# Sharing the last shifted reading of the exponential between VectorE and GpSimd, with other planner constants and another tail, in a one-core transformer block

## The chip, the core and the metric

The kernel runs on one core of a Trainium2 chip. The time is device microseconds (us) of the core for one execution, here the median of 3 runs. Engines: TensorE (PE in the profile), VectorE (DVE), ScalarE (ACT), GpSimd (POOL) and SyncE (SP), which issues the DMAs.

## What is computed

One block with adaptive layer norm: 2048 rows of 512, 32 heads of 16, then a dense layer of 1376 with gelu. Inputs are bf16.

```python
mod = (silu(c) @ w_mod).reshape(1, 6, 1, 512)   # sa, ca, ga, sb, cb, gb
h = layernorm(x) * (1 + ca) + sa
q, k, v = heads(h @ wqkv)                        # 32 heads of 16
p = softmax(q k^T / 4)
x = x + ga * ((p v) @ wo)
h = layernorm(x) * (1 + cb) + sb
x = x + gb * (gelu(h @ w1 + b1) @ w2 + b2)
```

## The kernel before

**Tiles.** The rows are cut into four blocks of 512 queries (`NQ`). Attention goes in 32 *runs*: a run is four heads with 512 queries in the first three blocks, and eight heads with 256 queries (two halves of 256 columns) in the last. A run walks over 16 tiles of 128 keys, and a tile has four *score pieces* of 128 keys x 512 columns, so there are 2048 score pieces in all. TensorE makes a piece in a quarter of its rows (L822).

**Two ways to an exponential.** Most pieces go to ScalarE: three pieces, then two, in turn, land in PSUM tiles `st` (one of three banks, one of two), and one exp instruction reads them all and writes `pt` (L871). For up to four key tiles of a run VectorE does it without an exp: a *PSUM pass* (L912) adds a constant to a score piece in PSUM tile `ax`, cuts it off at zero and writes it as int16 into a quarter of `ph`; its bits, read as bf16, are a coarse power of two. Four *shifts* (L927) add a constant to the whole of `ph` (128x2048, int16, SBUF to SBUF) into `sh`. The V product (L960) sums the five readings, each with V scaled to match (`VX`, made by GpSimd in L756), which evens out the coarseness. The four passes and four shifts of one key tile are called a group here. The sum lands in `od`, with a column of ones giving the denominators; VectorE copies it to SBUF (`OD`, L985), the denominators go through DRAM and come back spread, and GpSimd multiplies (L1012).

**What sets the order.** The order of every engine's instructions is found while the program is built, by a planner (`Plan`, L105) that plays the engines forward with a cost for each operation. It picks for each engine the ready operation with the best priority, and which key tiles go to VectorE (`next_tile`, L801) falls out of that. Its constants are the costs: `A_US` (an exp of one, two or three pieces), `AL` (from an exp's cost to the release of its banks), `PEL` (from the matmul's cost to its readers), and `SEEDS`, which breaks near ties, one for every 25 us of planned time. `ahead` (L162) keeps out TensorE work that would make ScalarE's next scores late. Nothing moves at run time: the chip follows these orders and waits on semaphores. An operation marked `port` uses the SBUF port that VectorE's SBUF-to-SBUF shifts and GpSimd are planned to take in turn; `beside` (L175, L1043) lets GpSimd work only while VectorE does something else, and `after_dve` (L1049) ties such a GpSimd instruction to the end of the VectorE instruction before the one last issued.

**Around attention.** `layer_norm` (L635) makes statistics on VectorE, the inverse deviation on GpSimd (L612, L614), and transposes on TensorE, one `ax` bank for each of four column blocks. `block_tail` (L1153) makes a block's output projection, residual, layer norm and dense layer beside the next runs; 11 blocks of 128 of the dense layer, one `ax` bank each (L1183), are moved out by VectorE (L1193) and put through one gelu. For the last block `block_tail` is called for the first 256 rows only. Eight of its dense blocks go that way and three wait for the end of all exps and are read by ScalarE (L1189). Two banks (`ax`) serve all this and VectorE's scores; the other banks are `od` and `st`.

**The tail.** When the last run ends, `last_half` (L1223) finishes the last 256 rows, two tiles of 128: it loads x again, and for each tile transposes `od`, inverts the denominators, multiplies (L1249 to L1256), projects (L1263), adds (L1267), and goes through layer norm (L607 to L618), the dense layer (L1295, L1298, L1123), the last add (L1310) and the store. The second tile's transposes use the same `OD` buffer and wait for the first tile's statistics.

Of the kernel before, what the change touches and what calls it, by code (L numbers as in the profile page):

```python
# [12 lines left out]
ALU = mybir.AluOpType  # L13
# [40 lines left out]
PEL = 0.24  # L54
OVER = 0.0
DVE_PE = 0.0
DL = 0.14
DPL = 0.08
AL = 0.17
FILL = 1.6  # L60
SPREAD = 0.15
SEEDS = (571, 338, 517, 702, 966, 607, 659, 937, 623, 185, 209, 513, 12, 512, 674, 785, 660, 579, 642, 245, 112, 195, 497, 319, 388, 80, 556, 716, 338, 990, 290, 195)
# [11 lines left out]
class Op:  # L74
    count = 0

    def __init__(self, eng, fn, us, deps=(), lat=0.14, prio=5.0, mode=None, kind="", acq=None,
# [10 lines left out]
        self.rows, self.cont, self.run = None, False, None  # L88
# [16 lines left out]
class Plan:  # L105
# [39 lines left out]
    def pick(self, eng):  # L145
# [4 lines left out]
        if eng == "PE":  # L150
            can = self.ahead(can)
# [10 lines left out]
    def ahead(self, can):  # L162
# [4 lines left out]
        limit = max(q[0][0], self.need() - q[0][1].us - PEL - 0.02) + OVER  # L167
# [5 lines left out]
        return keep  # L173

    def beside(self, us):  # L175

        at, end, port = self.dve
        t = max(at, self.now, self.free["POOL"])
        if t >= end:
            nxt = self.pick("DVE")  # L180
            return nxt is None or nxt[0] - t >= us
        return not port and end - t >= us

# [74 lines left out]
def kernel(  # L258
# [34 lines left out]
    MM = 512 / 2400.0  # L293
    SPAN = (3, 2)
    POOL_US, POOL_MIN = 0.68, 0.5
    A_US = {1: 0.49, 2: 0.92, 3: 1.345}
    AHEAD = 3
    PSUM_F = 8
# [50 lines left out]
    def dyn(plan, o):  # L349
        if o.eng == "DVE" and o.run is not None and (  # L350
                o.run < a_run[0] or o.run == a_run[0] and not own[o.run]):
            return 0.05
        if o.eng != "PE":
            return o.prio
# [14 lines left out]
        if o.kind == "last":  # L369
            return o.prio + 0.1 * same  # L370
        if o.due <= prog():
# [263 lines left out]
    def layer_norm(src, deps, mod, mod_dep, hold_z, alloc_h, engines, ps_res, kind, prio,  # L635
# [39 lines left out]
        else:  # L675
            for j in range(NC):
                def tr(o, j=j):
                    o.ps = o.tile.bitcast(BF16)[:, 0:nt * P]
                    for t in range(nt):
                        nc.tensor.transpose(out=o.ps[:, t * P:(t + 1) * P],  # L680
                                            in_=z.tile[:, t, j * P:(j + 1) * P], identity=ident)
                one = op("PE", tr, nt * 0.0705, za, lat=PEL, mode=("full", 0), kind=kind,
                         acq=r_ax, rel=(z,))
                trs.append(one)
                e = engines[j]
                done.append(op(e, lambda o, j=j, one=one, e=e: modulate(
                    e, h.tile[:, j, 0:nt * P], one.ps, mod, j), 0.13 + nt * 0.1, (one, mod_dep, h), prio=0.1,
                    rel=(one,)))
# [144 lines left out]
    def qk_a():  # L833
# [30 lines left out]
        o = op("PE", go, MM, deps, lat=PEL, mode=("qk",) + tuple(u[2] for u in got), kind="qkA", acq=r_st[n],  # L864
# [19 lines left out]
    def qk_d():  # L884
# [29 lines left out]
        d_e.append(op("DVE", ex, 0.61, (o,), lat=DL, prio=0.5, rel=(o,)))  # L914
# [7 lines left out]
    def shifts(r, kt, first, es):  # L922
# [3 lines left out]
        for j in range(1, NPH):  # L926
# [4 lines left out]
            pv_op(r, kt, j, (sh,), parts(sh), (sh,))  # L931

# [50 lines left out]
    def normalise(r):  # L983
# [20 lines left out]
        def d5(o):  # L1004
# [8 lines left out]
            out=OT.tile[:, c], in0=OD.tile[:, c], in1=o5.tile[:, c], op=ALU.mult), (OT,), (OD, o5))  # L1013
# [29 lines left out]
    def beside(fn, deps, rel=(), prio=0.5):  # L1043

        return [op("POOL", lambda o, c=c: after_dve(fn(slice(c * HB, (c + 1) * HB))), POOL_US, deps, lat=0.1,
# [107 lines left out]
    def block_tail(b, nt=TPB):  # L1153
# [19 lines left out]
        if part:  # L1173
            g.uses += 1
            o_late["part"] = g
            one = ones(g, (g,))
        ev = []
        over = op("NIL", None, 0.0, (), lat=0.0, prio=0.0, gate=finished) if part else None
        if part:
            open_banks()  # L1180
        for f in range(NF):
            direct = part and f >= PSUM_F
            mm = chain([(lambda ps, f=f, j=j: nc.tensor.matmul(  # L1183
                out=ps[:, 0:N], lhsT=W1[:, j, f * P:(f + 1) * P], rhs=h.tile[:, j, 0:N],
                start=(j == 0), stop=(j == NC - 1)), nt * MM / NC) for j in range(NC)],
                hd + [o_late["w1"], g, over if direct else None], kind,
                r_t if direct else r_ax, (h,))
            if direct:
# [264 lines left out]
```

## Time and profile before

| What | Value |
|---|---|
| Runs | 788.44 us median, 787.47 to 790.36 |
| Span of the profiled execution, first to last instruction | 785.5 us |
| Median of the runs less that span | 2.9 us |
| Mean granted TensorE clock | 0.996 |
| Busy: PE / DVE / ACT / POOL | 731.1 (93%) / 737.5 (94%) / 756.9 (96%) / 125.0 (16%) us |
| First exp starts, last exp ends | 14.2, 761.0 us |
| Chain that ended last, by engine | ACT 42%, PE 29%, DVE 14%, issue 12%, DMA 2% |

The profile is of one execution. Its own time is its span and what lies around it, which the profile does not give; the median of the runs is the nearest figure. A line of it names the source line, the engine, the operation, the tiles written and read with their shapes and how many there were; then busy time, mean duration in ns, and the idle time of the engine just before these instructions with what ended it. A mean duration runs from an instruction's start to its end, and on VectorE and ScalarE the next one starts before that, so what a long row costs is read from starts, not from means. PE's busy time is modelled and says little of how much room it has.

### The profile page before, as it was taken

The numbers are of one execution on the slowest core, as the hardware profiler recorded it, in microseconds if no ns is written. First come the engines' busy times: TensorE is split into PE (matmuls) and PEld (weight loads), VectorE is DVE, ScalarE is ACT, GpSimd is POOL, SyncE is SP. The second block draws the span as 40 slices with busy tenths as digits, with TensorE's granted clock in tenths as the row PEclk, the third lists the DMA queues.
The fourth block names the chain that finished last, engine by engine and source line by source line (L and its number), as shares of the span: only waits on it lengthen the run. The fifth ranks groups of instructions, "written<-read, shape, count | busy, mean of one in ns | idle before, by whom it ended". The sixth has DMA issues, their size and how long they took to land.

```text
span 785.5 us, 20448 instructions
## 1 busy us (share of the span) xinstructions
PE 731.1 (93%) x8209; PEld 272.8 (35%) x8286; DVE 737.5 (94%) x1285; ACT 756.9 (96%) x683; POOL 125.0 (16%) x279
## 2 busy tenths in 40 slices
PE   8899999999999898999998999999999999999897
PEld 3423333233333222223232233322234343344454
DVE  6779998999999999999999999999899999999974
ACT  4899999999999999999999999999999999999993
POOL 7420224121134300200002000001000100100100
PEclk9999999999999999999999999999999999999999
DMA  7042001001020010001000010001010000101010
GB/s 215 30 138 89 18 23 46 23 16 26 6 71 22 25 42 23 19 22 29 22 23 18 30 34 22 11 16 33 23 57 20 22 20 19 43 18 31 18 44 29
DMA packets 39073, 28.22 MB, mean 36 GB/s; under 512 B 17957, under 2 KB 34374, under 8 KB 38978
## 3 DMA queue, kind: packets, MB, share of 16 engines
q1 hardware_dynamic: 38970, 26.91, 12.0%
q8 instruction: 65, 1.06, 0.6%
q14 instruction: 30, 0.25, 0.1%
q10 hardware_dynamic: 8, 0.00, 0.0%
HBM read 21.30 MB, written 2.61 MB: 30 GB/s over the span
## 4 chain that ended last, share of the span: by engine, by line
ACT 42%; PE 29%; DVE 14%; issue 12%; DMA 2%; SPq 0%; POOL 0%; POOLq 0%; DVEq 0%; ACTq 0%
ACT pt L871 40%; PE od L960 9%; PE st L822 8%; DVE sh L927 6%; DVE ph L912 5%; PE ax L1123 2%; PE ax L822 2%; PE ax L1183 2%; ACT g L1202 1%; PE ax L701 1%; PE ax L431 1%; PE ax L740 1%; DVE ln_s L607 1%; DVE OD L985 1%; PE t L1123 1%
## 5 line engine op out<-in xcount | busy, mean ns | idle before, releaser
L871 ACT ACTIVATE pt<-st 128x1536 bf16<-128x1536 f32 x629 | 715.1, 1308 | 3.9 <-PE ax L822 1.7
L912 DVE TENSOR_SCALAR ph<-ax 128x512 int16<-128x512 f32 x476 | 311.1, 680 | 11.2 <-PE ax L822 9.7
L927 DVE TENSOR_SCALAR sh<-ph 128x2048 int16<-128x2048 int16 x476 | 310.8, 692 | 2.6 <-PE od L960 2.3
L822 PE MATMUL st<-qm,kT 32*128 32x512 bf16 x1572 | 246.8, 384 | 23.9 <-ACT pt L871 18.7
L822 PE MATMUL ax<-qm,kT 32*128 32x512 bf16 x476 | 167.0, 380 | 7.6 <-DVE ph L912 5.6
L960 PE MATMUL od<-sh,VX 128*32 128x512 bf16 (+1 forms) x2400 | 167.5, 340 | 5.4 <-DVE sh L927 4.6
L822 PEld LDWEIGHTS <-kT 32*128 32x128 bf16 x2048 | 81.1, 91 | 239.4 <-issue 230.6
L960 PE MATMUL od<-pt,VEB 128*32 128x512 bf16 (+1 forms) x1960 | 145.3, 342 | 0.3 <-ACT pt L871 0.3
L960 PEld LDWEIGHTS <-VX 128*32 128x32 bf16 x2400 | 60.5, 95 | 86.2 <-issue 75.3
L960 PEld LDWEIGHTS <-VEB 128*32 128x32 bf16 x2560 | 62.5, 96 | 75.6 <-issue 63.8
L1012 POOL TENSOR_TENSOR OT<-OD,RB 128x256 bf16<-128x256 f32 x38 | 27.2, 727 | 316.3 <-DVE sh L927 200.4
L960 PE MATMUL od<-ph,VEB 128*32 128x512 bf16 (+1 forms) x600 | 47.5, 340 | 1.7 <-DVE OD L985 1.4
L1012 POOL TENSOR_TENSOR OS<-OD,RB 128x256 bf16<-128x256 f32 x24 | 17.2, 727 | 156.7 <-DVE sh L927 111.0
L1183 PE MATMUL ax<-blk,W 128*128 128x512 bf16 (+1 forms) x145 | 39.8, 359 | 1.8 <-issue 0.6
L756 POOL TENSOR_SCALAR VX<-VEB 128x128 bf16<-128x128 bf16 x64 | 23.1, 360 | 80.7 <-DVE VEB L633 76.9
L701 PE MATMUL ax<-blk,w 128*128 128x512 bf16 x95 | 31.8, 382 | 3.7 <-DVE blk L626 0.9
L1123 PE MATMUL ax<-w,g 128*128 128x512 bf16 x100 | 29.2, 382 | 1.0 <-DVE ph L912 0.2
L1193 DVE TENSOR_SCALAR g<-ax,b1c 128x512 bf16<-128x512 f32 (+1 forms) x41 | 28.2, 692 | 1.1 <-PE ax L1183 0.7
L607 DVE BATCH_NORM_STATS2 ln_s<-xb 128x6 f32<-128x512 bf16 x32 | 21.6, 675 | 1.2 <-DMA xb<-in_A_x_dram 1.1
L1123 PEld LDWEIGHTS <-g 128*128 128x128 bf16 x176 | 14.0, 97 | 23.2 <-issue 12.7
L985 DVE COPY OD<-od 128x512 f32<-128x512 f32 x31 | 21.1, 681 | 0.7 <-issue 0.5
L1183 PEld LDWEIGHTS <-W 128*128 128x128 bf16 x176 | 14.0, 97 | 20.6 <-issue 14.9
(110 smaller groups left out, 367.5 us busy)
## 6 DMA issues: line engine op xcount, KB each, us to landing
RB<-rn SPq DMA_DIRECT2D x124, 64.0 KB
xb<-in_A_x_dram SPq DMA_DIRECT2D x8, 512.0 KB
out_dram<-o SPq DMA_DIRECT2D x16, 128.0 KB
qm<-qs SPq DMA_DIRECT2D x120, 16.0 KB
W<-in_B_w_dram SPq DMA_DIRECT2D x1, 1376.0 KB
w<-in_A_wqkv_dram SPq DMA_DIRECT2D x3, 384.0 KB
blk<-in_w_mod_dram SPq DMA_DIRECT2D x2, 512.0 KB
xb<-in_w_mod_dram SPq DMA_DIRECT2D x2, 512.0 KB
```

Of the source, the lines that this page charges most:

```text
L607: nc.vector.bn_stats(out=st6, in_=src)
L701: return chain([(lambda ps, j=j: nc.tensor.matmul(out=ps[:, 0:QB], lhsT=w.tile[:, j, cc * P:(cc + 1) * P], rhs=o_h[b].tile[:, j, :], start ...
L822: nc.tensor.matmul(out=o.tile[:, k * QB:(k + 1) * QB], lhsT=kT[cc][kb][rows, ko * P:(ko + 1) * P], rhs=qm.tile[rows, par, :] if hb is None ...
L871: nc.scalar.activation(out=e.tile[:, 0:len(got) * QB], in_=o.tile[:, 0:len(got) * QB], func=ACT.Exp, scale=ESC)
L912: nc.vector.tensor_scalar(out=ph.tile[:, o.row * QB:(o.row + 1) * QB], in0=o.tile, scalar1=PH_B, scalar2=0.0, op0=ALU.add, op1=ALU.max)
L927: sh = op("DVE", lambda o, j=j: nc.vector.tensor_scalar(out=o.tile, in0=first.tile, scalar1=PH_SH[j], scalar2=None, op0=ALU.add), 0.6, es, ...
L960: nc.tensor.matmul(out=o_od[r].tile[32 * i:32 * i + 32, n * HB:n * HB + w], lhsT=v_tile(kt, ph)[:, c0:c0 + 32], rhs=got[i][:, at:at + w], ...
L985: OD = op("DVE", lambda o: nc.vector.tensor_copy(out=o.tile, in_=od.tile), 0.6, (last,), prio=0.0, acq=r_OD, rel=(od,))
L1012: two = beside(lambda c: nc.gpsimd.tensor_tensor(out=OT.tile[:, c], in0=OD.tile[:, c], in1=o5.tile[:, c], op=ALU.mult), (OT,), (OD, o5))
L1123: nc.tensor.matmul(out=ps, lhsT=g[:, f, col:col + P], rhs=rhs, start=(f == 0), stop=(f == NF - 1))
L1183: mm = chain([(lambda ps, f=f, j=j: nc.tensor.matmul(out=ps[:, 0:N], lhsT=W1[:, j, f * P:(f + 1) * P], rhs=h.tile[:, j, 0:N], start=(j == ...
L1193: ev.append(op("DVE", lambda o, f=f, mm=mm: nc.vector.tensor_scalar(out=g.tile[:, f, 0:N], in0=mm.tile[:, 0:N], scalar1=b1c[:, f:f + 1], s ...
```

## The change

- Three of the four shifts of a group stay as they are. The last is shared (`shared_reading`): four candidates of 512 columns are offered to GpSimd, and the rest, whatever is left when VectorE reaches it, to VectorE. The V product of that reading waits for all parts. A piece is planned at 0.86 us, and `fits` admits it only when VectorE's present and next operation leave the port free for 0.8 us.
- Planner constants: `AL` 0.17 to 0.055, a new `PEA` of 0.38 in place of `PEL` for ScalarE's scores, exps of two and three pieces 0.9165 and 1.3435, `MM` 0.2155, 32 other seeds; chains once begun get a higher priority (`cont`).
- `fed`: TensorE work that would let VectorE run out of score pieces is kept back.
- `layer_norm` and `block_tail` put two (or four) blocks into one `ax` bank, where their size allows it.
- The last block's first half sends all 11 dense blocks through VectorE and gelu in SBUF (two blocks, then nine in one instruction); the three that ScalarE read from PSUM are gone.
- `last_half` keeps the x tile that the first half loaded, in place of loading it again, and takes an `OD` buffer for each tile, without the wait for the first tile's statistics. The last tiles' second dense layer goes to an `ax` bank.
- The normalising products of the last run but one may run at any time, not only beside VectorE.

The diff, cut to its core:

```diff
-AL = 0.17
+PEA = 0.38
+AL = 0.055
+FEED = 0.2
...
+    def fed(self, can):
+        q = [(s, o) for s, o in can if o.kind == "qkD"]
+        if not q:
+            return can
+        dry = self.free["DVE"] + sum(o.us for o in self.lists["DVE"])
+        limit = max(q[0][0], dry - q[0][1].us - PEL - DL) + FEED
+        return [(s, o) for s, o in can if o.kind in ("qkA", "qkD") or
+                s + o.us + (0.107 if o.mode[0] != "qk" else 0.0) <= limit]
...
+    def fits(self, us):
+        at, end, port = self.dve
+        t = max(at, self.now, self.free["POOL"])
+        if port and t < end:
+            return False
+        nxt = self.pick("DVE")
+        if nxt is None or nxt[0] - t >= us:
+            return True
+        if t >= end or nxt[0] > end + 0.15:
+            return not nxt[1].port and nxt[0] + nxt[1].us - t >= us
+        return end - t >= us or not nxt[1].port and nxt[0] + nxt[1].us - t >= us
...
-    MM = 512 / 2400.0
+    MM = 0.2155
-    A_US = {1: 0.49, 2: 0.92, 3: 1.345}
+    A_US = {1: 0.49, 2: 0.9165, 3: 1.3435}
+    PIECE = 0.86
+    REST = (4.0, 1.0)
+    PIECE_FIT = 0.8
...
-        for j in range(1, NPH):
+        shared_reading(r, kt, first, es)
+        for j in range(1, NPH - 1):
...
+    def shared_reading(r, kt, first, es):
+        sh = op("NIL", None, 0.0, es, lat=0.0, prio=0.0, acq=r_sh)
+        todo = [0, 1, 2, 3]
+        done = Op("NIL", None, 0.0, (), lat=0.0, prio=0.0, rel=(first,))
+        done.todo = 1
+        def add(eng, n):
+            at = slice(todo[0] * QB, (todo[0] + n) * QB)
+            del todo[:n]
+            return eng.tensor_scalar(out=sh.tile[:, at], in0=first.tile[:, at], scalar1=PH_SH[-1],
+                                     scalar2=None, op0=ALU.add)
+        def part(o):
+            after_dve(add(nc.gpsimd, 1))
...
+        def rest(o):
+            o.us = (0.067, 0.2, 0.335, 0.47, 0.6)[len(todo)]
+            o.waiters.append(done)
+            add(nc.vector, len(todo))
+            drop()
...
+        mine = [op("POOL", part, PIECE, (sh,), lat=0.12, prio=0.8, kind="beside", port=True,
+               gate=lambda: plan.fits(PIECE_FIT)) for _ in range(4)]
+        q = op("DVE", rest, 0.6, (sh,), lat=DL, prio=2.0, port=True)
...
+        pv_op(r, kt, NPH - 1, (done,), src, (sh,))
...
-            direct = part and f >= PSUM_F
...
+        for f0 in range(0, NF, QB // N):
+            fs = range(f0, min(NF, f0 + QB // N))
...
-        xr = load_x(b)
+        x2 = held["x"]
...
-        od, OD, OT = o_od[r], take(r_OD), take(r_OT)
+        od, OT = o_od[r], take(r_OT)
...
+            OD = take(r_OD)
...
-                    (o_last[r], OD, s), prio=0.06 + n)
+                    0.42, (o_last[r], OD), lat=0.03, prio=0.06 + n)
...
-                       kind="last", acq=r_t if f == 0 else None, prio=0.4)
+                       kind="last", acq=r_ax if f == 0 else None, prio=0.4)
```

Line numbers move in the changed kernel: the exp is L903, the PSUM pass L944, a whole shift L960, the shared reading L976, the V product L1036.

## The prediction

> **What bounds the kernel now.** First view: the page's slices, engine by engine, with the costliest groups.
>
> ```profile
> DVE  6779998999999999999999999999899999999974
> ACT  4899999999999999999999999999999999999993
> POOL 7420224121134300200002000001000100100100
> ...
> L871 ACT ACTIVATE pt<-st 128x1536 bf16<-128x1536 f32 x629 | 715.1, 1308 | 3.9 <-PE ax L822 1.7
> L912 DVE TENSOR_SCALAR ph<-ax 128x512 int16<-128x512 f32 x476 | 311.1, 680 | 11.2 <-PE ax L822 9.7
> L927 DVE TENSOR_SCALAR sh<-ph 128x2048 int16<-128x2048 int16 x476 | 310.8, 692 | 2.6 <-PE od L960 2.3
> ...
> L1012 POOL TENSOR_TENSOR OT<-OD,RB 128x256 bf16<-128x256 f32 x38 | 27.2, 727 | 316.3 <-DVE sh L927 200.4
> ```
>
> The reader is to see three things. ScalarE's exps (L871) fill 715.1 us with 3.9 us of idle time before them. VectorE's share, PSUM passes (L912) and shifts (L927), fills 622 us. GpSimd is nearly empty after a third of the span. Second view: the busy time of each engine by stretch of the span (columns: length, PE, PEld, DVE, ACT, POOL).
>
> ```profile
> 300.00:400.00 100.00, 92.82 (x913) 29.34 (x921) 99.12 (x172) 99.75 (x89) 9.84 (x14) 1.00 0.09 24
> 500.00:600.00 100.00, 93.98 (x1032) 31.51 (x1046) 95.69 (x160) 98.77 (x84) 6.48 (x9) 1.00 0.10 29
> 760.00:785.50 25.50, 20.20 (x191) 12.16 (x186) 10.41 (x24) 12.90 (x34) 1.77 (x5) 1.00 0.14 44
> ```
>
> Over 40 to 760 us the idle times of ScalarE in these stretches add up to 3.0 us. The last exp ends at 761.0, and a tail of 24.5 us follows in which ScalarE and VectorE are half empty. So the end is set by the front, the length of ScalarE's queue of exps, its gaps, and the tail; VectorE is close behind in the middle.
>
> **Exps.** The built order, which holds no times, has 484 PSUM passes (476 before), so 8 score pieces leave ScalarE: 313 exps of 1536 columns, 312 of 1024 and one of 512, against 314 and 315. ScalarE's own price, from its order in time:
>
> ```profile
> 700.23 60.76 ACT L871 ACTIVATE pt<-st 128x1536 bf16<-128x1536 f32 x53 [0.31 <-PE ax L822]
> ```
>
> 53 exps, wide and narrow in turn: (60.76 - 1.52) / 26 = 2.28 us a pair; two other such rows give 2.27 and 2.28. (The means of one, 1.520 and 1.096, overlap.) With 1.520 - 1.096 = 0.424 for 512 columns, an exp costs 1.35, 0.93 or 0.50 us. One wide and three narrow go, one of 512 comes: -1.35 - 2.78 + 0.50 = **-3.6 us**. Other ScalarE work ahead of the tail is unchanged. The front is not touched: both orders are the same through the tenth exp.
>
> **VectorE.** Shifts and passes follow each other every 0.60 us. Of 121 groups, 363 shifts stay whole. The 121 last readings are split so: VectorE makes all of 57, three quarters of 22, half of 12, a quarter of 8, none of 22; GpSimd makes 158 pieces. Whole shifts go from 476 to 420: -33.6. 42 part shifts come; they are not in the trace. Between their share of 0.60 (14.7 in all) and 0.60 each (25.2), I take the planner's 0.47, 0.335 and 0.2, 16.0 us, which lies by the share. 8 more passes: +4.8. Net -12.8 us (-14.1 to -3.6). On the path this is worth nothing, since ScalarE ends last; it is what pays for the 8 score pieces and for collisions.
>
> **A piece on GpSimd** (512 columns, int16, one input) is not in the trace either. The nearest rows are these: a stretch in order of time on GpSimd and on VectorE, and two lines' shortest, median and longest times in ns (the count at the end of such a row is of records with a shape and may be short).
>
> ```profile
> 155.24 0.73 POOL L1012 TENSOR_TENSOR OT<-OD,RB 128x256 bf16<-128x256 f32 x1 [16.53 <-DVE sh L927]
> ```
> ```profile
> 155.07 0.68 DVE L912 TENSOR_SCALAR ph<-ax 128x512 int16<-128x512 f32 x1
> 155.68 0.84 DVE L927 TENSOR_SCALAR sh<-ph 128x2048 int16<-128x2048 int16 x1
> ```
> ```profile
> L756 POOL TENSOR_SCALAR VX<-VEB x64: 300/301/741, 16.4 to 231.7; 128x128 bf16<-128x128 bf16 x64
> ```
> ```profile
> L927 DVE TENSOR_SCALAR sh<-ph x476: 622/682/1228, 45.4 to 757.5; 128x2048 int16<-128x2048 int16 x159
> ```
>
> 128 columns take 0.301 and two columns (L612) 0.22, so 512 take 0.54 if the growth goes on, and 1.20 if all of it scales by four. I take 0.86, the planner's own price, near the 0.73 of the row that also reads 512 columns. The first three lines show the danger: GpSimd starts 0.17 us after the pass it goes beside, outlasts it, and the next shift takes 0.84 in place of 0.68. The extremes say the same: a GpSimd scaling of 0.30 has taken 0.74, a shift 1.23. What guards against it is in the built order: no piece has fewer than two VectorE instructions other than shifts (and layer norm's applies) between its place and the next shift. 68 have just two, a window of 1.20, of which 1.03 is left after the start. A piece of 0.86 fits and costs VectorE nothing; one of 1.20 costs 68 x 0.17 = 11.6 us, all that was freed. Behind a piece on GpSimd's own queue stand the normalising products and the layer norms' rstd; it idles hundreds of us before them, so nothing is late. The V product of a shared reading waits for its last piece, and on TensorE the next scores for ScalarE stand behind that.
>
> The Trainium skill, "GPSIMD Engine Reference", opening and section 3.1, speaks against the change: GpSimd is the wrong choice for ordinary elementwise work, and its best one-input loop takes 769 ns for 512 elements. No row here shows that loop. By it the piece would be 0.77, inside the window, and the sum the same. "SBUF — State Buffer", section "Who interferes with whom", says the port shared with VectorE is held for the whole instruction and the other blocks fully. By that the shift above should lose 0.17 + 0.73 - 0.60 = 0.30; it lost 0.16, so a collision costs about half as much here.
>
> **Planner's other constants** (exp to release 0.17 to 0.055, scores to exp 0.24 to 0.38, the rule that keeps VectorE fed, chains with two blocks to a bank, seeds). They add no instruction and reorder TensorE. The trace shows ScalarE waiting for scores seven times, 3.2 us, of which 3.0 of idle time from 40 us on, and TensorE waiting for an exp 67 times, 18.7 us. An order that places scores 0.14 earlier can at best remove the 3.0. At worst gaps come all over as they do from 500 to 700 us (1.9 us in 200): 6.9 over 720 us, +3.9. I take 0, between the two.
>
> **Tail.** These lines of the order in time carry it.
>
> ```profile
> 761.54 0.45 DVE L1249 STREAM_TRANSPOSE OD<-od 128x256 f32<-128x256 f32 x1 [2.52 <-issue]
> ...
> 766.59 0.69 DVE L1267 TENSOR_TENSOR xb<-t,xb 128x512 bf16<-128x512 f32 x1 [3.42 <-DMA xb<-in_A_x_dram]
> ...
> 775.93 2.80 PE L1295 MATMUL t<-blk,W 128*128 128x128 bf16 x44
> ...
> 782.06 0.69 DVE L1310 TENSOR_TENSOR o<-t,xb 128x512 bf16<-128x512 f32 x1 [1.74 <-PE t L1123]
> ```
>
> The first tile's residual add waits 3.42 us for x, which is loaded again; the change keeps x. The second tile's transposes need no longer wait for the first tile's statistics. Against that, 11 first-layer matmuls (0.107 each from a 256-column row's spacing, 1.2 us) now stand ahead of the last V product, which starts the chain about 0.5 us later after the last exp, and the gelu of nine blocks is one instruction: 1.47 + 768 x 0.82 ns = 2.1 us (0.82 ns a column from the 512- and 1536-column gelus, 0.63 and 1.47), with TensorE idle about 1 us before the 9 matmuls that need it. Placing the built order at these rows, counted from the end of the last exp: the first add starts at 3.7 (before 5.6), the second tile's at 9.5 (10.7). Then TensorE is what is late: 22 second-layer matmuls of the first half at 0.213, the first tile's 44 at 0.064 and the rest are in front. The second tile's 44 start at 14.6 (14.9), and 12 second-layer matmuls in place of 15 follow them: -0.3 - 0.6 = **-1.0 us** (0, if nothing passes TensorE, to -1.8, the second add's whole 1.2 and the three matmuls).
>
> **Sum.** 785.5 - 3.6 - 1.0 = 780.9 us of span. The runs' median is 788.44, 2.9 above that span; I keep the 2.9: **783.8 us**, 0.6% below.
>
> **Rivals.** *A, gaps on ScalarE eat it.* The order is new everywhere after the front; at the rate of 500 to 700 us it has +3.9, and with no gain in the tail +1.0: 788.7; with half of each, 786.2. For: one blocked TensorE instruction holds all behind it. Against: 0.4 us of gaps in 400 us from 100 to 500. *B, pieces longer than the plan (slower).* Place: the V product that waits for a shared reading. A piece of 1.20 is 0.34 over 0.86; behind four in a row the product is 1.36 late, and ScalarE holds about one exp in hand, 0.93. So 22 readings of four lose 0.43 each and 8 of three 0.09: 10.2 us, 794.0. It is slower by over 0.5% when 22 (4d - 0.93) + 8 (3d - 0.93) passes 8.6 us, that is from d = 0.33, a piece of 1.19. For: VectorE's and GpSimd's collisions in the trace. Against: the 0.73 row. *C, better than the sum.* Gaps fall to the 100 to 500 rate (0.7 us, so -2.3) and the tail gives 1.8 in place of 1.0: 780.7. That the change does nothing is excluded by the built order, which has the pieces.
>
> **How the numbers follow.** What a measurement of this kernel can tell from no change is about 0.5%, 3.9 us: faster is below 784.5, slower above 792.4. The forecast case (782 to 785.5) has 0.45, of which a quarter lies over 784.5; A 0.17; B 0.14, with 0.01 of other mishaps beside it; C 0.23. Faster: 0.34 + 0.23 = 0.57. Same: 0.11 + 0.17 = 0.28. Slower: 0.15. The range goes from 779.5 (C and a little) to 792.5, which leaves most of B out.
>
> **What would show it.** Right: VectorE's row of passes x484, GpSimd's pieces x158 at 0.75 to 0.95 us, exps about 711.5 us busy with under 5 us of idle before them, the last exp's end near 757.4, a tail of 23.5. Wrong: pieces over 1.1 us; TensorE waiting long for GpSimd; shifts with a mean well over 0.70 us; ScalarE idle by over 7 us between 40 us and its last exp; a tail as long as before.

## The result, and the profile after

The changed kernel takes **828.98 us** (median of 4 runs, 825.40 to 832.04) against 789.40 us for the kernel before (4 runs, 787.47 to 792.68): a ratio of **1.0493**, with a 95% interval of 1.0453 to 1.0533. The forecast was 783.8 us, and its range ended at 792.5. The profiled execution took 825.40 us with a span of 823.6, so 1.8 us lie around the span.

The page's slices of VectorE, ScalarE and GpSimd show it at a glance: ScalarE's row, which had nines from the third slice to the last but one, has seven eights now, VectorE's has twelve eights in place of two, and GpSimd's is some 40% full nearly to the end.

```profile
DVE  6789889999999898999998899988989999989984
ACT  4989989999999998999998999988999999899994
POOL 7452365341567553462256257444511646741430
```

These are the costliest groups of the changed kernel, which answer to the lines shown of before (L903 for L871, L944 for L912, L960 for L927, L1088 for L1012), with the new ones.

```profile
L903 ACT ACTIVATE pt<-st 128x1536 bf16<-128x1536 f32 x626 | 716.9, 1279 | 43.3 <-PE ax L854 27.1
L944 DVE TENSOR_SCALAR ph<-ax 128x512 int16<-128x512 f32 x484 | 315.6, 682 | 42.0 <-PE ax L854 35.7
L976 POOL TENSOR_SCALAR sh<-ph 128x512 int16<-128x512 int16 x158 | 249.2, 1594 | 183.1 <-DVE sh L960 89.5
...
L960 DVE TENSOR_SCALAR sh<-ph 128x2048 int16<-128x2048 int16 x363 | 255.1, 737 | 1.4 <-PE od L1036 0.7
L1036 PE MATMUL od<-sh,VX 128*32 128x512 bf16 (+1 forms) x2432 | 185.4, 345 | 30.8 <-POOL sh L976 22.3
...
L1088 POOL TENSOR_TENSOR OT<-OD,RB 128x256 bf16<-128x256 f32 x38 | 29.1, 781 | 82.9 <-DVE sh L960 48.7
```

The third line holds the answer: a piece on GpSimd lasts about 1.5 us, not 0.86. Its shortest, median and longest times, in ns, are in the first line of the view of its source line; the second line is VectorE's rest of the same reading.

```profile
L976 POOL TENSOR_SCALAR sh<-ph x158: 1482/1489/2280, 52.8 to 784.3; 128x512 int16<-128x512 int16 x158
L976 DVE TENSOR_SCALAR sh<-ph x99: 277/683/1159, 46.6 to 794.0; 128x2048 int16<-128x2048 int16 x57, 128x1536 int16<-128x1536 int16 x22, 128x1024 int16<-128x1024 int16 x12, 128x512 int16<-128x512 int16 x8
```

The shortest is 1.482 us and the median 1.489, so 1.49 is the price of the instruction itself. Some were held up as well: the mean is 1594 ns, and 51 of the 158 last over 1.54 us. Two more things stand in the groups. Whole shifts grew from a mean of 692 to 737 ns. TensorE, which before waited for no piece of GpSimd, now waits 22.3 us for one, at the V product. ScalarE's idle time before exps went from 3.9 to 43.3 us, VectorE's before passes from 11.2 to 42.0. Both wait for scores. The stretches that were shown of before read so now (length, PE, PEld, DVE, ACT, POOL, then the granted clock):

```profile
300.00:400.00 100.00, 90.50 (x894) 27.83 (x892) 93.72 (x160) 93.82 (x83) 44.82 (x40) 0.98 0.10 27
500.00:600.00 100.00, 92.46 (x838) 25.71 (x836) 91.60 (x152) 90.55 (x76) 51.98 (x39) 0.95 0.08 18
```

ScalarE was busy 99.75 and 98.77 in these before; it is 93.82 and 90.55 now, and no engine is full. One such hole, in the timeline of all engines (start, length, what, and in brackets the idle time before it and what ended it):

```profile
210.06 9.34 POOL L976 TENSOR_SCALAR sh<-ph 128x512 int16<-128x512 int16 x6 [3.48 <-DVE ph L944]
...
216.55 0.38 PE L1036 MATMUL od<-sh,VX 128*32 128x512 bf16 x1 [1.21 <-POOL sh L976]
...
216.86 0.39 PE L854 MATMUL st<-qm,kT 32*128 32x512 bf16 x3
216.87 0.38 PE L854 MATMUL ax<-qm,kT 32*128 32x512 bf16 x1
...
217.33 0.69 DVE L944 TENSOR_SCALAR ph<-ax 128x512 int16<-128x512 f32 x1 [1.30 <-PE ax L854]
217.35 2.37 ACT L903 ACTIVATE pt<-st 128x1536 bf16<-128x1536 f32 x2 [1.70 <-PE ax L854]
```

GpSimd makes six pieces back to back, 9.34 / 6 = 1.56 us each. The V product that needs the fourth waits 1.21 us (210.06 + 4 x 1.56 = 216.3). The next scores stand behind it in TensorE's queue: those for ScalarE and those for VectorE. When both start again 0.8 us later, they have been idle for 1.30 and 1.70 us. This is the place that Rival B named.

The tail did what was forecast, and a little more. The last 16 exps are one row of ScalarE's timeline:

```profile
782.73 18.10 ACT L903 ACTIVATE pt<-st 128x1536 bf16<-128x1536 f32 x16 [0.19 <-PE st L854]
```

The last exp ends at 782.73 + 18.10 = 800.8, and the span at 823.6: 22.8 us, against 24.5 before. These lines of VectorE's timeline and of TensorE's answer to those of before.

```profile
804.85 0.65 DVE L1345 TENSOR_TENSOR xb<-t,xb 128x512 bf16<-128x512 f32 x1
...
810.21 0.68 DVE L1345 TENSOR_TENSOR xb<-t,xb 128x512 bf16<-128x512 f32 x1
```
```profile
814.83 2.62 PE L1373 MATMUL t<-blk,W 128*128 128x128 bf16 x44
```

Nothing waits for x any more. Counted from the last exp's end, the first add starts at 4.0 us, the second at 9.4, the second tile's 44 matmuls at 14.0.

### The profile page after: what moved, and what is told of

It reads as the page before. It is cut to its first block, busy times and chain, and to the rows that moved or that the text cites. A ratio compares the mean times of both kernels' runs of the same rounds, so it can differ in the third digit from the quotient of the medians.

```text
span 823.6 us, 20793 instructions
## 1 busy us (share of the span) xinstructions
PE 755.4 (92%) x8318; PEld 270.3 (33%) x8318; DVE 746.2 (91%) x1282; ACT 758.3 (92%) x677; POOL 375.6 (46%) x437
## 4 chain that ended last, share of the span: by engine, by line
PE 32%; DVE 26%; ACT 16%; POOL 14%; issue 8%; DMA 2%; SPq 0%; DVEq 0%; POOLq 0%; ACTq 0%
ACT pt L903 15%; POOL sh L976 13%; PE od L1036 12%; DVE ph L944 10%; DVE sh L960 9%; PE st L854 8%; PE ax L1202 4%; PE ax L854 2%; DVE sh L976 2%; PE ax L1263 2%; PE ax L733 1%; DMA dc<-dn 1%; DVE g L1268 1%; DVE OD L1061 1%; DMA blk<-in_w_mod_dram 1%
## 5 line engine op out<-in xcount | busy, mean ns | idle before, releaser
L903 ACT ACTIVATE pt<-st 128x1536 bf16<-128x1536 f32 x626 | 716.9, 1279 | 43.3 <-PE ax L854 27.1
L944 DVE TENSOR_SCALAR ph<-ax 128x512 int16<-128x512 f32 x484 | 315.6, 682 | 42.0 <-PE ax L854 35.7
L976 POOL TENSOR_SCALAR sh<-ph 128x512 int16<-128x512 int16 x158 | 249.2, 1594 | 183.1 <-DVE sh L960 89.5
L960 DVE TENSOR_SCALAR sh<-ph 128x2048 int16<-128x2048 int16 x363 | 255.1, 737 | 1.4 <-PE od L1036 0.7
L1036 PE MATMUL od<-sh,VX 128*32 128x512 bf16 (+1 forms) x2432 | 185.4, 345 | 30.8 <-POOL sh L976 22.3
L854 PEld LDWEIGHTS <-kT 32*128 32x128 bf16 x2048 | 76.8, 91 | 241.4 <-issue 232.7
L1036 PE MATMUL od<-pt,VEB 128*32 128x512 bf16 (+1 forms) x1952 | 146.3, 345 | 0.2 <-DVE OD L1061 0.2
L1036 PEld LDWEIGHTS <-VX 128*32 128x32 bf16 x2432 | 62.0, 95 | 112.6 <-issue 103.1
L1036 PEld LDWEIGHTS <-VEB 128*32 128x32 bf16 x2560 | 64.9, 97 | 78.6 <-issue 66.0
L1088 POOL TENSOR_TENSOR OT<-OD,RB 128x256 bf16<-128x256 f32 x38 | 29.1, 781 | 82.9 <-DVE sh L960 48.7
L976 DVE TENSOR_SCALAR sh<-ph 128x2048 int16<-128x2048 int16 (+3 forms) x99 | 63.9, 655 | 2.1 <-PE od L1036 2.1
L1036 PE MATMUL od<-ph,VEB 128*32 128x512 bf16 (+1 forms) x608 | 50.8, 347 | 0.7 <-DVE OD L1061 0.4
L1263 PE MATMUL ax<-blk,W 128*128 128x512 bf16 (+1 forms) x176 | 45.7, 361 | 1.8 <-DVE ph L944 1.2
L1088 POOL TENSOR_TENSOR OS<-OD,RB 128x256 bf16<-128x256 f32 x24 | 17.1, 727 | 57.7 <-DVE sh L960 31.8
L733 PE MATMUL ax<-blk,w 128*128 128x512 bf16 x124 | 36.5, 382 | 2.4 <-DVE blk L658 0.9
L1202 PE MATMUL ax<-w,g 128*128 128x512 bf16 x128 | 35.1, 381 | 1.4 <-DVE ph L944 1.0
```

Source lines behind the costliest of these rows:

```text
L733: return chain([(lambda ps, j=j: nc.tensor.matmul(out=ps[:, 0:QB], lhsT=w.tile[:, j, cc * P:(cc + 1) * P], rhs=o_h[b].tile[:, j, :], start ...
L854: nc.tensor.matmul(out=o.tile[:, k * QB:(k + 1) * QB], lhsT=kT[cc][kb][rows, ko * P:(ko + 1) * P], rhs=qm.tile[rows, par, :] if hb is None ...
L903: nc.scalar.activation(out=e.tile[:, 0:len(got) * QB], in_=o.tile[:, 0:len(got) * QB], func=ACT.Exp, scale=ESC)
L944: nc.vector.tensor_scalar(out=ph.tile[:, o.row * QB:(o.row + 1) * QB], in0=o.tile, scalar1=PH_B, scalar2=0.0, op0=ALU.add, op1=ALU.max)
L960: sh = op("DVE", lambda o, j=j: nc.vector.tensor_scalar(out=o.tile, in0=first.tile, scalar1=PH_SH[j], scalar2=None, op0=ALU.add), 0.6, es, ...
L976: return eng.tensor_scalar(out=sh.tile[:, at], in0=first.tile[:, at], scalar1=PH_SH[-1], scalar2=None, op0=ALU.add)
```

## The experiments

**The theory** from this profile was that a long piece holds the V product, and behind it the scores of both engines. The rivals were that the planner's new order is to blame, and that the loss comes from GpSimd's long pieces blocking VectorE's shifts at the shared port.

**First three kernels: shorter pieces, pieces that nobody waits for, no pieces.** The edits to the changed kernel, each alone (tiles made apart for the readings in the first two are left out):

```diff
 # e1_short
+            if eng is nc.gpsimd:
+                at = slice(at.start, at.start + 64)
 # e2_spare
+            if eng is nc.gpsimd:
+                return eng.tensor_scalar(out=SPARE[0], in0=first.tile[:, at], scalar1=PH_SH[-1],
+                                         scalar2=None, op0=ALU.add)
 # e3_none
-               gate=lambda: plan.fits(PIECE_FIT)) for _ in range(4)]
+               gate=lambda: plan.fits(PIECE_FIT)) for _ in range(0)]
```

> The changed kernel's order of instructions, with GpSimd writing only the first 64 columns of each 512-column piece (the other columns of the reading stay as an earlier reading left them, so the output is not the reference's); every wait is kept. Theory (the pieces take 1.49 us where the planner and I had 0.86, and the V product that waits for them holds TensorE's queue and with it ScalarE): the time falls to the forecast, 781 to 787 us. Rival 1 (the new order itself, from the other constants and the rule that feeds VectorE, leaves ScalarE without scores): it stays above 815. Rival 2 (collisions on the shared port): also near 784, since a short piece collides with little; the next kernel tells it apart.

> The changed kernel's order, with each piece written at full length into a spare tile that nothing reads; the V products read what the shared tile held before (the output is not the reference's), so they wait for no piece, while GpSimd works as long and at the same places. Theory (the wait is what costs): most of the 39 us goes, 785 to 800; the shifts that GpSimd blocks keep their mean of about 0.74 us. Rival 2 (the blocked shifts are what costs): it stays above 815. Rival 1 (the order): above 815 too.

> The change without pieces: no candidate is offered to GpSimd, VectorE makes the whole last reading, and the planner orders anew with all other constants of the change and the new tail. Theory: no GpSimd wait is left, ScalarE's idle time before exps falls from 43 to under 8 us and the time to 783 to 791. Rival 1 (the other constants): ScalarE still idles 30 us or more and the time is above 810.

Measured: e1_short 786.69 us, ratio 0.9955 (0.9928 to 0.9983), with 2.1 us of idle time before exps. e2_spare 815.87, 1.0349 (1.0304 to 1.0394), with 25.3 us idle and whole shifts at a mean of 739 ns. e3_none 800.34, 1.0136 (1.0108 to 1.0164), with 12.3 us idle.

The first held: it is the length of the pieces. The second went against the theory, which had given most of the loss to the wait of the V product: without that wait more than half of it is still there, and the shifts are as long as in the changed kernel. The third, at 800.34, fits neither what the theory expected nor what the rival did, and was hard to read. All three had other orders than the changed kernel: 476, 476 and 464 passes in place of 484, and in the first two 171 and 136 pieces in place of 158. The planner breaks near ties by a hash that takes in the line number of each operation's function, and added lines move these. From here on the edits kept every line in its place, and the four kernels that follow have the changed kernel's order exactly (in e5 to e7 the readings' tiles are made apart, a line that is left out here; e8 keeps them where they were).

**The same order, four kinds of piece.**

```diff
 # e5_short_same: a piece writes 64 columns
-            at = slice(todo[0] * QB, (todo[0] + n) * QB)
+            at = slice(todo[0] * QB, todo[0] * QB + (64 if eng is nc.gpsimd else n * QB))
 # e6_spare_same: a full piece into a tile that nobody reads
-            return eng.tensor_scalar(out=sh.tile[:, at], ...
+            return eng.tensor_scalar(out=SPARE if eng is nc.gpsimd else sh.tile[:, at], ...
 # e7_four_short: 64 columns, four times over
+            return [eng.tensor_scalar(out=sh.tile[:, at], ...) for _ in range(4 if eng is nc.gpsimd else 1)][0]
 # e8_int32: the same sums, two 16-bit numbers in one 32-bit add
+            K102 = const.tile([P, 1], I32, name="k102"); nc.gpsimd.memset(K102, PH_SH[-1] * 65537)
...
+            return eng.tensor_tensor(out=sh.tile[:, at].bitcast(I32), in0=first.tile[:, at].bitcast(I32),
+                                     in1=K102.to_broadcast([P, QB // 2]), op=ALU.add) if eng is nc.gpsimd else ...
```

> The changed kernel's order, instruction by instruction and line by line, with GpSimd writing only the first 64 columns of each of the 158 pieces (the rest of the reading is left from an earlier one, so the output is not the reference's); all waits are kept. It is the short-piece run again, since that one's added lines had moved the planner's tie breaks, which hang on line numbers (171 pieces in place of 158). Theory (all of the loss hangs on the length of a piece): the forecast's own sum without its mistake, 781 to 787 us, ScalarE idle under 5 us before its exps. Rival (the order leaves gaps by itself): above 790.

> The changed kernel's exact order; each piece goes at full length to a spare tile, so that no V product waits for GpSimd (the output is not the reference's), and only the port is held as long. Theory 1 (the port: a piece of 1.49 us blocks shifts, VectorE falls behind and its late scores and readings hold TensorE's queue): 808 to 825. Theory 2 (TensorE's wait for the pieces): 785 to 800.

> The changed kernel's exact order; each piece is four instructions of 64 columns in a row (the same columns four times, the output is not the reference's), some 1.47 us of GpSimd time in all, so that the V product waits about as long as for a piece of 1.49, but the port is given back every 0.37 us. Theory 1 (the port): under 800, the shifts' mean back to about 0.70 us. Theory 2 (the wait): above 815. If both count, between.

> The changed kernel's exact order, with the whole computation: a piece adds 102 to 512 int16 numbers as an int32 add of 256 columns (102 in both halves; no carry passes between them, since all are under 32768). From the 0.67 to 0.73 us of the two-input rows with 256 columns I expect 0.65 to 0.80 a piece, less than the planner's 0.86. Theory (length of a piece): 781 to 787 us, faster than before. If a piece is again over 1.2 us: above 800.

Measured:

| Kernel | us | Ratio to before | Piece, ns (median) | Whole shift, mean ns | Idle before exps | V product waits for GpSimd |
|---|---|---|---|---|---|---|
| e5_short_same | 780.47 | 0.9894 (0.9860 to 0.9927) | 368 | 692 | 3.9 | none listed |
| e8_int32 | 782.13 | 0.9893 (0.9860 to 0.9925) | 611 | 691 | 3.9 | none listed |
| changed kernel | 828.98 | 1.0493 (1.0453 to 1.0533) | 1489 | 737 | 43.3 | 22.3 |
| e6_spare_same | 806.10 | 1.0199 (1.0164 to 1.0234) | 1489 | 754 | 21.6 | cannot |
| e7_four_short | 879.55 | 1.1123 (1.1066 to 1.1181) | 4 of 368 | 700 | 91.7 | 50.8 |

Two of the four lie in the range of an expectation: e8 (with a piece shorter than the 0.65 to 0.80 us expected) and e7, which is above the 815 of its second theory. e5 is half a microsecond under its range, and e6 lies between its two, near the lower end of the port's.

e5 against the changed kernel: the same instructions in the same order, only GpSimd's shorter, and the whole 48.5 us are gone. e6 splits them. With long pieces that nothing waits for, 806.10 - 780.47 = **25.6 us** remain, and these come by way of the shared port or what follows from it: the one other wait for GpSimd that grew is VectorE's for the layer norms' deviation, which stands behind pieces in GpSimd's queue, from 3.5 us in e5 to 5.5. Its lines:

```profile
L976 POOL TENSOR_SCALAR spare<-ph 128x512 int16<-128x512 int16 x158 | 256.7, 1625 | 178.3 <-DVE shk L960 99.2
...
L960 DVE TENSOR_SCALAR shk<-ph 128x2048 int16<-128x2048 int16 x363 | 262.0, 754 | 2.2 <-PE od L1036 1.6
L1036 PE MATMUL od<-shk,VX 128*32 128x512 bf16 (+1 forms) x2432 | 175.5, 342 | 16.3 <-DVE shk L960 13.1
```

VectorE is busy 754.0 us in e6 and 725.7 in e5, 28.3 more in a span that is 26.5 longer: here VectorE is the bound. The other 22.9 us of the changed kernel come when its V products do wait. The books of VectorE's own two numbers close in the same way. From e5 to the changed kernel its busy time grows by 20.5, nearly all in the shifts, its idle time before passes by 42.0 - 19.1 = 22.9, together 43.4 of the span's 45.0.

e7 is the other side of the trade. In four short instructions GpSimd gives the port back in between, so shifts stay near 700 ns. But shifts now get in between the four, and what VectorE no longer loses the pieces lose: single instructions up to 1432 ns, and a V product that waits more than in the changed kernel.

```profile
PE od L1036 <- POOL shk L976: 50.8, 41, 2.3
PE st L854 <- ACT pt L903: 11.9, 43, 0.8
PE ax L854 <- DVE ph L944: 7.7, 22, 1.1
```

(The waits of TensorE in e7: total us, times, longest.) With these waits, in a queue that feeds two engines, the kernel is 99 us slower than e5. Not all of it need be the wait: the granted clock of TensorE was 0.943 in e7 and 0.996 in e5, and TensorE was busy 783.0 us with matmuls that took it 733.7 in e5.

e8 makes the whole computation, with pieces of 0.61 us. It beats both kernels, by 0.75 to 1.40% the kernel before. These are its lines.

```profile
L903 ACT ACTIVATE pt<-st 128x1536 bf16<-128x1536 f32 x626 | 710.0, 1337 | 3.9 <-PE ax L854 2.5
...
L960 DVE TENSOR_SCALAR sh<-ph 128x2048 int16<-128x2048 int16 x363 | 238.7, 691 | 1.4 <-PE od L1036 0.7
...
L976 POOL TENSOR_TENSOR sh<-ph,k 128x256 int32<-128x256 int32 x158 | 95.8, 611 | 252.4 <-DVE sh L960 127.2
```

**The plan with the true price.** If the planner is told what a piece costs, does it find a use for them? And what does it do with the cheap form?

```diff
 # e9_priced
-    PIECE = 0.86
+    PIECE = 1.49
-    PIECE_FIT = 0.8
+    PIECE_FIT = 1.4
 # e10_int32_062: the pieces of e8, and
-    PIECE = 0.86
+    PIECE = 0.62
-    PIECE_FIT = 0.8
+    PIECE_FIT = 0.6
 # e11_line: the kernel before, with one empty line more above the planner
+
```

> The changed kernel with the measured price of a piece in the planner, 1.49 us, and 1.4 us asked for before one is let in. The planner then lets in 8 pieces in place of 158, and ScalarE gets 316 exps of each width. Theory (the price was the mistake): the 5% loss is gone, 786 to 801 us, no better than without pieces; TensorE waits under 3 us for GpSimd. Rival (pieces cost by something other than their length, such as the order around them): still above 805.

> The int32 add as a piece, with its measured price in the planner (0.62 us, and 0.6 us asked for): 239 pieces in place of 158, the same 484 passes, VectorE's whole shifts 397 in place of 420. Theory (ScalarE sets the end, and its work is the same): 779 to 788 us, the same as with 158 pieces within 0.5%, though VectorE's work falls by some 7 us; the seeds were chosen for another order, so a gap or two more on ScalarE would not surprise. Rival (VectorE sets the end): 772 to 776.

> The kernel before with one empty line put in above the planner and nothing else. The tie breaks hang on line numbers, so the order is another: 464 passes in place of 476, 12 score pieces back on ScalarE (+5.4 us by its prices). It measures what an order is worth that the seeds were not chosen for, and so whether the 800 us of the version without pieces says anything of the constants. Theory (it is the order): 792 to 803 us. Rival (the constants of the change slow it): 787 to 790, as before.

Measured: e9_priced 794.63, 1.0083 (1.0058 to 1.0108); the plan lets in 8 pieces and makes 468 passes. e10_int32_062 785.97, 0.9971 (0.9948 to 0.9995); 239 pieces, 484 passes; in its profiled execution, the slowest of the 12 (793.43 us), ScalarE idles 12.4 us before exps. e11_line 795.74, 1.0098 (1.0063 to 1.0133), with 464 passes in place of 476.

e11 is the measure of the others. It computes and plans with the same constants as the kernel before, and the order alone costs it 5 to 10 us (0.63 to 1.33%), since the seeds were chosen for one set of line numbers. The empty line also moves 12 score pieces back to ScalarE, which is part of what another order means here. So e3 and e9, which are also orders for which no seeds were chosen, say only that without useful pieces the new constants are about where any such order is, and nothing finer. e10 lies in its range, but 0.8% above e8 by their ratios and not within the 0.5% expected; it doesn't tell whether 239 pieces are too many or its order is a poor draw: open.

**The price of the form by itself.** After the end of the kernel before, with VectorE idle, GpSimd runs scratch operations, each list twice.

```diff
+    for _ in range(2):
+        gp.tensor_scalar(out=v(pb, 512), in0=v(pa, 512), scalar1=102, scalar2=None, op0=ALU.add)
+        gp.tensor_scalar(out=v(pb, 256), in0=v(pa, 256), scalar1=102, scalar2=None, op0=ALU.add)
+        gp.tensor_scalar(out=v(pb, 128), in0=v(pa, 128), scalar1=102, scalar2=None, op0=ALU.add)
+        gp.tensor_scalar(out=v(pb, 512), in0=v(pa, 512), scalar1=102, scalar2=0, op0=ALU.add, op1=ALU.add)
+        gp.tensor_scalar(out=v(pb, 512, BF16), in0=v(pa, 512, BF16), scalar1=2.0, scalar2=None, op0=ALU.mult)
+        gp.tensor_scalar(out=v(pb, 512, BF16), in0=v(pa, 512, BF16), scalar1=2.0, scalar2=0.0, op0=ALU.mult, op1=ALU.add)
+        gp.tensor_tensor(out=v(pb, 256, I32), in0=v(pa, 256, I32), in1=v(pc_, 256, I32), op=ALU.add)
+        gp.tensor_tensor(out=v(pb, 512, BF16), in0=v(pa, 512, BF16), in1=v(pc_, 512, BF16), op=ALU.add)
```

> The kernel before, with GpSimd instructions on scratch tiles behind its end, when VectorE does nothing: the int16 add of a constant on 512, 256 and 128 columns, the same with a second operation, a bf16 product on 512 columns with one and with two operations, an int32 add of two tensors on 256 columns, a bf16 add of two tensors on 512. Theory (1.49 us is the int16 operation's own price): 1.48 to 1.50 alone on 512 columns, about 0.85 on 256, 0.53 on 128, as 0.37 for 64 and 1.49 for 512 give. Rival (1.49 is a wait for the port): 0.8 to 0.9 alone. The bf16 forms I expect near 0.55, from 0.30 for 128 columns and 0.22 for two.

The second pass through the list, in GpSimd's timeline, in the order of the code:

```profile
797.55 1.49 POOL L1430 TENSOR_SCALAR sh<-ph 128x512 int16<-128x512 int16 x1
799.13 0.85 POOL L1431 TENSOR_SCALAR sh<-ph 128x256 int16<-128x256 int16 x1
800.06 0.53 POOL L1432 TENSOR_SCALAR sh<-ph 128x128 int16<-128x128 int16 x1
800.67 1.93 POOL L1433 TENSOR_SCALAR sh<-ph 128x512 int16<-128x512 int16 x1
802.68 1.50 POOL L1434 TENSOR_SCALAR sh<-ph 128x512 bf16<-128x512 bf16 x1
804.27 0.62 POOL L1435 TENSOR_SCALAR sh<-ph 128x512 bf16<-128x512 bf16 x1
804.97 0.72 POOL L1436 TENSOR_TENSOR sh<-ph,sh 128x256 int32<-128x256 int32 x1
805.77 1.15 POOL L1437 TENSOR_TENSOR sh<-ph,sh 128x512 bf16<-128x512 bf16 x1
```

1.49 needs no contention: it is what 512 columns with one operation cost on an idle port, in int16 (an add) as in bf16 (a product, 1.50). The fifth and sixth lines are the surprise: one operation on bf16 takes 1.50, two operations on the same data 0.62.

**The plan's own price, put to the test.** The last kernel cuts the piece to 256 columns, which the probe shows at 0.85: the figure that plan and prediction used, in the changed kernel's exact order. Was the price the whole error, or is 0.86 too long already?

```diff
-            at = slice(todo[0] * QB, (todo[0] + n) * QB)
+            at = slice(todo[0] * QB, todo[0] * QB + (256 if eng is nc.gpsimd else n * QB))
```

> The changed kernel in its exact order, each GpSimd piece cut to 256 of its 512 columns (the other half is left out), so that a piece lasts 0.85 to 0.87 us, the price that the plan and the prediction used. Theory (the error was the price of the piece alone, and the plan's window rule works at the price it was made for): 781 to 785 us, ratio 0.989 to 0.995, ScalarE idle before exps under 6 us, shifts at a mean of 690 to 700 ns. Rival (0.86 is already too long: pieces outlast the windows of two passes often enough): over 788 us, shifts over 705 ns, the V product waiting for GpSimd for more than 5 us.

Measured: **781.94 us**, 0.9912 (0.9882 to 0.9942), with these lines:

```profile
L903 ACT ACTIVATE pt<-st 128x1536 bf16<-128x1536 f32 x626 | 710.6, 1318 | 4.1 <-PE ax L854 2.5
...
L960 DVE TENSOR_SCALAR shk<-ph 128x2048 int16<-128x2048 int16 x363 | 239.9, 695 | 1.4 <-PE od L1036 0.7
L976 POOL TENSOR_SCALAR shk<-ph 128x256 int16<-128x256 int16 x158 | 133.5, 854 | 229.1 <-DVE shk L960 103.3
```

At 0.85 the collisions cost VectorE (695 - 692) x 363 = 1.1 us in its whole shifts, and TensorE waits for a piece once, for 0.2 us. The price of the piece was the whole error. In one order, pieces of 0.37, 0.61 and 0.85 give 780.5, 782.1 and 781.9; pieces of 1.49 give 829.0. The knee is between 0.85 and 1.49; where, was not tried.

## Why the prediction was wrong, step by step

**A piece on GpSimd: this step failed.** The prediction took 0.86 us "near the 0.73 of the row that also reads 512 columns", with 0.54 and 1.20 as bounds; it measured 1.49, outside both. The bound of 1.20 came from "if all of it scales by four", from the 0.301 of the `VX` row. That row is another form: the scaling of V (L756) has two operations, times and plus, and the piece has one. The probe and that row show both: two operations on bf16 go from 0.301 at 128 columns to 0.62 at 512, one operation on int16 from 0.53 to 1.49. A bound drawn from another form is not a bound. The piece's form differed in the number of operations and in the type, and the prediction named only the second as not in the trace. The lower reckoning mixed two forms: its 0.22 for two columns (L612) is an add with one operation, its 0.301 has two.

The trace of before does hold the piece's form, in float32 and on few elements: L612 adds one constant to two columns, and L570, one instruction on 4 partitions at the start, adds one constant to 128.

```profile
L570 POOL TENSOR_SCALAR ce<-ce x1: 538/538/538, 4.4 to 4.4; 4x128 f32<-4x128 f32 x1
L612 POOL TENSOR_SCALAR rs<-mv x17: 217/218/662, 5.6 to 773.4; 128x2 f32<-128x2 f32 x15, 128x1 f32<-128x1 f32 x2
```

From 0.218 at two columns to 0.538 at 128 is 2.54 ns a column, and 510 columns more than two give 0.218 + 1.295 = 1.51 us. That is an estimate over a change of type and of partitions, but it was there to be made, and it lies within 0.03 of the 1.49. The prediction overlooked this row. With 1.51 its own formula for Rival B would have forecast a slower kernel.

The Trainium skill, "GPSIMD Engine Reference", section 4.1, calls one-input work on GpSimd roughly line-rate, and section 3.1 has 769 ns for 512 elements of the best loop. The runs here show 1.49 us for one operation, 0.62 for two on bf16, so neither figure is a price for this form; the advice of its opening, not to use GpSimd for elementwise work, held for this form. e8, with another form, is faster than the kernel before, but no run here makes e8's readings on VectorE in the same order, so what GpSimd brings by itself isn't shown.

**Rival B's mechanism was right in its place, and counted half of the loss.** Its formula at d = 1.49 - 0.86 = 0.63 gives 22 x (2.52 - 0.93) + 8 x (1.89 - 0.93) = 42.7 us, and 783.8 + 42.7 = 826.5 would look like a hit on 829.0. It isn't, and its nearness is luck. The trace shows 22.3 us of TensorE's waiting at that product, not 42.7, and e6 loses 25.6 us without any such wait. It had a chance of 0.14, for a price that it put at 1.20.

**Collisions: the price was too low, and it hid in the piece.** The prediction read from one pair that a collision costs "about half" of the overlap. Two pairs of the changed kernel, with a shift that starts late in a piece, say nearly all of it. GpSimd's timeline, and VectorE's:

```profile
99.58 1.49 POOL L976 TENSOR_SCALAR sh<-ph 128x512 int16<-128x512 int16 x1 [1.30 <-DVE sh L960]
...
111.18 1.49 POOL L976 TENSOR_SCALAR sh<-ph 128x512 int16<-128x512 int16 x1 [0.26 <-DVE ph L944]
```
```profile
100.70 0.92 DVE L960 TENSOR_SCALAR sh<-ph 128x2048 int16<-128x2048 int16 x1
...
112.23 1.60 DVE L960 TENSOR_SCALAR sh<-ph 128x2048 int16<-128x2048 int16 x2
```

The first piece ends at 101.07, 0.37 after the shift starts. That shift takes 0.92, and its twin in e5, which has the same order, 0.62: 0.30 lost of 0.37. The second ends at 112.67, 0.44 into a pair of shifts that take 1.60, and in e5 1.28: 0.32 lost. VectorE's timeline of e5:

```profile
100.34 0.62 DVE L960 TENSOR_SCALAR shk<-ph 128x2048 int16<-128x2048 int16 x1
...
108.18 1.28 DVE L960 TENSOR_SCALAR shk<-ph 128x2048 int16<-128x2048 int16 x2
```

So here about 0.1 of an overlap is free and the rest is paid, which also fits the pair of before (0.16 lost of 0.30).

But a shift that starts earlier in a piece can pass it. GpSimd's timeline and VectorE's, of the changed kernel:

```profile
78.13 2.04 POOL L976 TENSOR_SCALAR sh<-ph 128x512 int16<-128x512 int16 x1 [1.48 <-DVE dc L1072]
```
```profile
79.02 0.68 DVE L960 TENSOR_SCALAR sh<-ph 128x2048 int16<-128x2048 int16 x1
```

This shift starts 0.89 after the piece and takes 0.68, as its twin in e5 does (at 78.66). It is the piece that waits: it lasts 2.04 in place of 1.49. Set against their twins in e5, the 108 shifts (L960, L976) that start while a piece runs lose 19.0 us. The 65 that start 0.92 or more after the piece lose 14.8 of them, the 28 that start at 0.45 to 0.92 only 0.5 (26 of these under 0.02 each), and the 15 that start before that 3.7. So a piece doesn't keep VectorE from the port from its start to its end; what goes on inside it isn't shown. "SBUF — State Buffer", section "Who interferes with whom", has the second engine blocked fully until the first is done. That is nearer to the late starts than the half that was set against it, and the starts at 0.45 to 0.92 show otherwise.

By the prediction's count, the 68 windows of two passes, with 1.03 left, would lose 0.46 - 0.1 each, 24 us. The shifts grew by 45 x 363 + 60 x 99 ns = 22.3 us. The sums are near, but the parts are not those 68 windows: 41 shifts start with over 0.2 us of a piece left and outlast it, and these lose 13.4 us.

**Exps: right.** Forecast 711.5 busy and a last end near 757.4. With pieces that fit, 710.6 busy (e14) and 734.38 + 22.61 = 757.0 in ScalarE's timeline. In the changed kernel itself the exps are busy 716.9; the busy time counts overlapping exps once, and there less overlaps (626 x 1.279 - 716.9 = 83.8 us, against 626 x 1.318 - 710.6 = 114.5 in e14).

**VectorE off the path: right at the price it was made for.** In e8 and e14 it is busy 726.0 and 727.7 us, ScalarE 751.3 and 751.9; against the 737.5 of before that is -11.5 and -9.8, for a forecast of -12.8. In the changed kernel 22.3 us of blocked shifts are more than that gain, and it was no cover any more.

**Planner's constants: 0 held.** In e5, e8 and e14 ScalarE's idle time before exps is 3.9 to 4.1 us, against 3.9 before. Rival A (gaps) is not seen in these three, and Rival C only in its tail.

**Tail: right in its mechanism, mis-sized.** Forecast -1.0 (its terms, -0.3 and -0.6, make -0.9), with -1.8 as the end of the range; measured 24.5 to 22.8, -1.7. The first two marks lay within 0.3 us of the forecast (first add 4.0 for 3.7, second 9.4 for 9.5); the 44 matmuls came at 14.0 in place of 14.6, so TensorE was less late than forecast.

**Sum.** With the error taken out, the forecast's span of 780.9 stands against 779.8 (e14) and 780.4 (e8), and most of the difference is the tail's 0.7. Adding 2.9 to the span was a little too much: the profiled execution has 1.8 around its span, the other profiled ones 1.7 to 1.9, and the other 1.1 was the draw of that one execution against the median.

**What stays open.** Why one operation on bf16 takes GpSimd 2.4 times as long as two, while on int16 two take longer than one (1.93 against 1.49). Whether more than 158 cheap pieces would pay, and what the pieces bring against VectorE making them all in an order as well chosen. What the lower granted clock adds. Runs of one kernel go with their clock: e8 from 777.82 us at 1.000 to 783.70 at 0.988, the changed kernel from 825.40 at 0.985 to 832.04 at 0.973, some 0.5 us for 0.001. By that slope, an estimate, the step from e5's 0.996 to 0.985 is worth some 5 us of the 45 between their spans, and that to e7's 0.943 some 25 of its 97. What lowers the clock, no run shows.

## What to carry to other kernels

A price extrapolated over a change of form (number of operations, type, one input or two) has no upper bound from the row that it came from; look in the source at what the row's instruction does, search the trace for a row of the same form, however small, and without one give the price a wide range. Work moved to an engine that is idle has two ways back to the path, the port that it shares and the consumer that waits for it, and both turn from nothing to tens of us once the piece outlasts its window; so find the window first and then ask which instruction form fits it. An experiment in a planned kernel must hold the order fixed, or its differences are the order's: one empty line, and the 12 fewer passes that came with it, cost 5 to 10 us here.

## What the runs showed of the hardware

- On GpSimd the form decides: adding one constant to 512 16-bit columns takes 1.49 us as a one-operation tensor_scalar, and 0.61 as an int32 tensor_tensor with a broadcast constant on 256 columns. Two operations cost 0.62 on bf16 and 1.93 on int16.
- A VectorE shift that starts 0.92 us or more after a GpSimd piece of 1.49 loses what is left of the piece but for about 0.1 us. One that starts at 0.45 to 0.92 loses next to nothing in 26 of 28 cases, and the piece waits for it (2.04 us in place of 1.49). Short instructions wait too: in e7, of 0.37 us, up to 1.43.
- A GpSimd instruction beside PSUM passes alone slows nothing that shows: 158 pieces of 0.61 us in e8 leave whole shifts at 691 ns and passes at 681.
